# Splitting every fourth V load by partitions, 112 + 8 + 8, in a grouped-query attention block

## The chip, the core and the metric

One core of one Trainium2 chip runs the whole program in one launch. The metric is the device time of that launch in microseconds (us). A run that is over 1.5% above the fastest of its kernel counts as slow. A profiled execution is a little shorter than its timed run, because its span runs from the first to the last instruction (385.4 us where the time was 387.23).

In a profile, PE is the matmul engine, PEld its weight load, DVE and ACT the two elementwise engines, SP the engine that issues nearly all the loads here. Sixteen DMA engines move the data.

## The reference

```python
# B=32, Sq=4, D=1024, Hq=32, Hkv=4, Sk=2048, Dh=128, all bf16
q = (x @ wq).reshape(B, Sq, Hq, Dh).transpose(0, 2, 1, 3)
k = repeat(k_cache, 8, axis=1); v = repeat(v_cache, 8, axis=1)
p = softmax(einsum("bhqd,bhkd->bhqk", q, k) * Dh ** -0.5)
o = einsum("bhqk,bhkd->bhqd", p, v)
return o.transpose(0, 2, 1, 3).reshape(B, Sq, Hq * Dh) @ wo
```

For each of the 32 batches 2 MB of K and 2 MB of V must come in from HBM, and 16 MB of weights besides: 151 MB in all, each byte used once.

## The kernel before

Each batch's K and V go into one of three buffers. A load is issued on SP as soon as the batch three earlier has let its buffer go, so several loads are queued at any time. In a V load partition p takes 16 consecutive keys of each of the four kv heads: four pieces of 4 KB. In a K load it takes one piece of 16 KB.

```python
def load_k(b):
    p.dma("sp", lambda e: e.dma_start(
        K_sb[:, b % NKB, :, :], k_cache[b].rearrange("g (r t) d -> (g r) t d", r=R)),
        [("fill", b - NKB, NFILL - 1)] if b >= NKB else [], ("k", b), f"s_k{b % NKB}")

def load_v(b):
    src = v_cache[b].rearrange("g (p t) d -> p g (t d)", p=128)
    dst = V_sb[:, b % NVB, :, :, :].rearrange("p g t d -> p g (t d)")
    waits = [("pv", b - NVB)] if b >= NVB else []
    if b < B - 1:
        p.dma("sp", lambda e: e.dma_start(dst, src), waits, ("v", b), f"s_v{b % NVB}")
    else:
        for g in range(G):   # the last one in four pieces, by head
            p.dma("sp", ..., waits, ("v", b, g), f"s_vl{g}")
# ... cut ...
load_k(0)
load_k(1)
for b in range(B):
    if b + 2 < B:
        load_k(b + 2)
    load_v(b)
    if b in (2, 3, 4, 5):
        load_wo(b - 2)
# ... cut: Q projection; per batch K transposes, QK, softmax, PV, output projection ...
```

A load's semaphore gets one increment from each DMA engine that worked on it, when that engine's share has landed. The consumer waits for the full count, so it waits for the slowest engine.

## Time and profile before

| | before |
|---|---|
| time | 387.33 us (387.23 to 387.41, 3 runs) |
| bytes moved | 152.32 MB, mean 395 GB/s |
| loads' share of the 16 DMA engines | 96.1% of the span |
| PE / DVE / ACT busy | 73% / 71% / 54% |
| DMA in the chain of waits | 59% |

The lines are from the page of the kernel before: the span; two rows of the 40 slices (9.6 us each; a digit is a busy share in tenths, the second row is what the DMA engines moved); the SP queue's packets, MB and share of 16 engines; the head of the chain of waits; and the DMA issues with KB of one load and median us from issue to landing.

```profile
span 385.4 us, 12595 instructions
DMA  7999999999999999999999999999999999999930
GB/s 328 432 432 416 418 417 398 413 410 395 413 409 409 419 416 414 419 413 418 417 419 417 417 414 417 416 416 411 417 417 417 418 420 415 417 418 410 375 143 9
...
q1 hardware_dynamic: 27104, 151.49, 96.1%
q8 instruction: 46, 0.75, 0.8%
...
DMA 59%; PE 17%; ACT 13%; DVE 7%; issue 2%; SPq 1%
...
K_sb<-in_k_cache_dram SPq DMA_DIRECT2D x32, 2048.0 KB, 25.4
V_sb<-in_v_cache_dram SPq DMA_DIRECT2D x31, 2048.0 KB, 27.3
```

The DMA row is full from the second slice to the 38th, at 375 to 432 GB/s. No compute engine is near full. The kernel is bound by its loads, and a load is on the way for 25 us, five loads' time: the queue is deep.

Behind these lines lie the single records. A V load costs an engine 32 packets of 4 KB at 161 ns, a K load 8 packets of 16 KB at 615 ns (26.6 GB/s for one engine). The times of the 16 increments of each semaphore show that the engines drift apart: the first and the last are 1.8 us apart in the first K load and 9.7 us in the last one. Eight engines fall behind, one at a time, in steps of about 1.5 us. The q8 line has 46 instruction packets of 16 KB, about six for each of the eight, and I read those as the steps' cause. The times bear this out: the lags of the engines behind the first one, added up, grow from 11.1 us when 5 instruction packets had started to 72.7 us when 42 had, about 1.7 us for each. The increments do not name their engine.

### The profile page before, as it was taken

Reading aid. Unit: us, or ns where it says so; the run is one execution under the profiler, and the core shown is the slowest. Engines: PE = TensorE matmul, PEld = TensorE weight load, DVE = VectorE, ACT = ScalarE, POOL = GpSimd, SP = SyncE. Lnnn points to the kernel's source line nnn. Section 1 sums busy time; section 2 is a strip of 40 time slices with the busy share of each in tenths; the row PEclk is TensorE's granted clock in tenths of the full one; section 3 lists DMA queues with packets and bytes.
Section 4 is the critical chain, followed back from the end, with each engine's and each line's share of the span. In section 5 each row is a group of like instructions: output and inputs, shape, how many; then the busy total and the mean of one; then the engine's idle time right before and its main releaser. Section 6 shows DMA issues by size and latency. Waiting matters only on the chain.

```text
span 385.4 us, 12595 instructions
## 1 busy us (share of the span) xinstructions
PE 280.9 (73%) x5929; PEld 229.5 (60%) x5929; DVE 274.1 (71%) x299; ACT 208.5 (54%) x261; POOL 0.7 (0%) x6
## 2 busy tenths in 40 slices
PE   1876888676383967888767778877767888776756
PEld 1875766465282856666655566665645676565545
DVE  0017999683552984899888859998868859987850
ACT  1005777355161646676666627766646566666620
POOL 0000000000000000000000000000000000000000
PEclk9998999886976899999999999999999999999978
DMA  7999999999999999999999999999999999999930
GB/s 328 432 432 416 418 417 398 413 410 395 413 409 409 419 416 414 419 413 418 417 419 417 417 414 417 416 416 411 417 417 417 418 420 415 417 418 410 375 143 9
DMA packets 27251, 152.32 MB, mean 395 GB/s; under 512 B 1472, under 2 KB 1984, under 8 KB 22592
## 3 DMA queue, kind: packets, MB, share of 16 engines
q1 hardware_dynamic: 27104, 151.49, 96.1%
q8 instruction: 46, 0.75, 0.8%
q10 hardware_dynamic: 96, 0.03, 0.0%
q14 instruction: 5, 0.04, 0.0%
HBM read 151.26 MB, written 0.26 MB: 393 GB/s over the span
## 4 chain that ended last, share of the span: by engine, by line
DMA 59%; PE 17%; ACT 13%; DVE 7%; issue 2%; SPq 1%
DMA K_sb<-in_k_cache_dram 59%; ACT KT_sb L219 7%; ACT P_sb L285 6%; DVE KT_sb L217 4%; PE ps_r L207 4%; PE ps_r L248 3%; PE ps_r L296 3%; PE ps_r L225 3%; PE ps_s L240 3%; DVE mx L280 2%; PE ps_s L296 1%; DVE PT_sb L231 0%; SPq L129 0%; PE ps_r L271 0%; ACT oT_sb L275 0%
## 5 line engine op out<-in xcount | busy, mean ns | idle before, releaser
L207 PE MATMUL ps_r<-ident,K_sb 128*128 128x128 bf16 x2048 | 142.6, 229 | 66.0 <-DMA K_sb<-in_k_cache_dram 40.8
L217 DVE COPY KT_sb<-ps_r 128x1024 bf16<-128x1024 bf16 x128 | 148.0, 1216 | 40.0 <-PE ps_r L207 39.8
L207 PEld LDWEIGHTS ps_r<-ident,K_sb 128*128 128x128 bf16 x2048 | 125.7, 103 | 82.2 <-DMA K_sb<-in_k_cache_dram 41.9
L219 ACT ACTIVATE KT_sb<-ps_r 128x1024 bf16<-128x1024 bf16 x128 | 124.5, 1025 | 72.1 <-PE ps_r L207 72.0
L280 DVE TENSOR_REDUCE mx<-ps_s 128x1 f32<-128x2048 f32 x32 | 73.3, 2292 | 7.1 <-PE ps_s L240 4.6
L285 ACT ACTIVATE P_sb<-ps_s,negmx 128x2048 bf16<-128x2048 f32 x32 | 63.0, 1969 | 2.2 <-DVE negmx L281 2.1
L231 DVE COPY PT_sb<-ps_r 128x1024 bf16<-128x1024 bf16 x64 | 41.4, 686 | 16.7 <-PE ps_r L225 15.2
L248 PE MATMUL ps_r<-V_sb,PT_sb 128*32 128x128 bf16 x2048 | 36.7, 223 | 17.2 <-ACT KT_sb L219 12.8
L248 PEld LDWEIGHTS ps_r<-V_sb,PT_sb 128*32 128x32 bf16 x2048 | 31.0, 98 | 22.7 <-ACT KT_sb L219 19.4
L275 ACT ACTIVATE oT_sb<-ps_r 128x128 bf16<-128x128 bf16 x31 | 8.6, 277 | 55.6 <-PE ps_r L271 55.6
L225 PE MATMUL ps_r<-ident,P_sb 128*128 128x128 bf16 x512 | 35.1, 223 | 1.8 <-ACT P_sb L285 1.4
L240 PE MATMUL ps_s<-KT_sb,QT_sb 128*32 128x512 bf16 x512 | 34.3, 386 | 2.5 <-DVE KT_sb L217 1.7
L225 PEld LDWEIGHTS ps_r<-ident,P_sb 128*128 128x128 bf16 x512 | 29.4, 99 | 5.4 <-ACT P_sb L285 1.6
L240 PEld LDWEIGHTS ps_s<-KT_sb,QT_sb 128*32 128x32 bf16 x512 | 10.8, 96 | 13.3 <-issue 2.8
L187 DVE CAST QT_sb<-ps_r 128x512 bf16<-128x512 f32 x2 | 1.3, 686 | 22.4 <-PE ps_r L176 22.4
L265 ACT ACTIVATE o_sb<-ps_r,rinv 128x128 bf16<-128x128 f32 x31 | 11.4, 367 | 9.8 <-PE ps_r L248 9.8
L189 ACT ACTIVATE QT_sb<-ps_r 128x512 bf16<-128x512 f32 x2 | 1.1, 594 | 26.0 <-PE ps_r L176 26.0
L176 PE MATMUL ps_s<-P_sb,w_sb 128*128 128x128 bf16 x128 | 9.4, 232 | 7.2 <-DMA w_sb<-in_wq_dram 7.2
L296 PE MATMUL ps_r<-w_sb,oT_sb 128*32 128x256 bf16 x384 | 11.5, 273 | 2.6 <-issue 1.4
L176 PEld LDWEIGHTS ps_s<-P_sb,w_sb 128*128 128x128 bf16 x128 | 8.3, 105 | 7.8 <-issue 4.4
L296 PEld LDWEIGHTS ps_r<-w_sb,oT_sb 128*32 128x32 bf16 x384 | 10.0, 97 | 3.7 <-issue 2.5
L271 PEld LDWEIGHTS ps_r<-ident,o_sb 128*128 128x128 bf16 x31 | 3.0, 98 | 12.7 <-issue 12.7
(30 smaller groups left out, 58.9 us busy)
## 6 DMA issues: line engine op xcount, KB each, us to landing
K_sb<-in_k_cache_dram SPq DMA_DIRECT2D x32, 2048.0 KB, 25.4
V_sb<-in_v_cache_dram SPq DMA_DIRECT2D x31, 2048.0 KB, 27.3
w_sb<-in_wq_dram SPq DMA_DIRECT2D x4, 2048.0 KB, 14.8
w_sb<-in_wo_dram SPq DMA_DIRECT2D x4, 2048.0 KB, 24.7
V_sb<-in_v_cache_dram SPq DMA_DIRECT2D x4, 512.0 KB, 15.8
P_sb<-in_x_dram SPq DMA_DIRECT2D x1, 256.0 KB, 2.8
out_dram<-y_sb SPq DMA_DIRECT2D x14, 16.0 KB, 12.1
out_dram<-y_sb ACTq DMA_DIRECT2D x2, 16.0 KB, 1.6
```

The source lines that it names most:

```text
L176: p.op("pe", lambda e, kt=kt, h=h: e.matmul(ps_q(h), lhsT=w_sb[:, kt, h * Dh:(h + 1) * Dh], rhs=xT_sb[:, kt, :], start=(kt == 0 and h % 4 ...
L207: p.op("pe", lambda e, q=q, t=t: e.transpose(buf[:, q * 128:(q + 1) * 128], K_sb[:, b % NKB, t, :], ident[:, :]), waits + [("k", b), "iden ...
L217: p.op("dve", lambda e: e.tensor_copy(dst, src), waits, ("kt", b, f))
L219: p.op("act", lambda e: e.activation(dst, src, ACT.Copy), waits, ("kt", b, f))
L225: p.op("pe", lambda e, q=q: e.transpose(buf[:, q * 128:(q + 1) * 128], P_sb[:, (8 * f + q) * 128:(8 * f + q + 1) * 128], ident[:, :]), wai ...
L231: p.op("dve", lambda e: e.tensor_copy(PT_sb[:, 8 * f:8 * f + 8, :].rearrange("p t q -> p (t q)"), buf), [("ptf", i, f)] + ([("pv", i - 1)] ...
L240: p.op("pe", lambda e, c=c, g=g: e.matmul(ps_s[32 * g:32 * (g + 1), c * 512:(c + 1) * 512], lhsT=QT_sb[:, i, REP * g:REP * (g + 1), :], rh ...
L248: p.op("pe", lambda e: e.matmul(buf[32 * g:32 * (g + 1), 0:Dh], lhsT=PT_sb[:, t, 32 * g:32 * (g + 1)], rhs=V_sb[:, i % NVB, g, t, :], star ...
L265: p.op("act", lambda e: e.activation(o_sb[:, :], buf[:, 0:Dh], ACT.Copy, scale=rinv[:, i:i + 1]), [("pv", i), ("rinv", i)] + ([("oT", i - ...
L280: p.op("dve", lambda e: e.tensor_reduce(mx[:, i:i + 1], ps_s[:, :], AX.X, ALU.max), [("qk", i)], ("mx", i))
L285: p.op("act", lambda e: e.activation(P_sb[:, :], ps_s[:, :], ACT.Exp, bias=negmx[:, i:i + 1], scale=scale, accum_out=ssum[:, i:i + 1]), [( ...
L296: p.op("pe", lambda e, h=h, j=j: e.matmul(buf[32 * j:32 * (j + 1), 0:NC], lhsT=oT_sb[:, h, 32 * n:32 * (n + 1)], rhs=wo_sb[:, h, NC * j:NC ...
```

## The change

Its evident intent is to level that drift. The split pieces of 8 rows run on 8 DMA engines instead of 16, so in each split load these 8 engines get 9 partitions each and the other 8 get 7, in place of 8 and 8.

```diff
+        v_parts = {}
+
         def load_v(b):
 ...
             if b < B - 1:
-                p.dma("sp", lambda e: e.dma_start(dst, src), waits, ("v", b), f"s_v{b % NVB}")
+                parts = ((0, 112), (112, 120), (120, 128)) if b % 4 == 2 else ((0, 128),)
+                for n, (p0, p1) in enumerate(parts):
+                    p.dma("sp", lambda e, p0=p0, p1=p1: e.dma_start(dst[p0:p1, :, :], src[p0:p1, :, :]),
+                          waits, ("v", b, n), f"s_v{b % NVB}_{n}")
+                v_parts[b] = [("v", b, n) for n in range(len(parts))]
 ...
         def pe_pv(i):
-            waits = waits + [("pt", i, 0), ("pt", i, 1), ("v", i)]
+            waits = waits + [("pt", i, 0), ("pt", i, 1)] + v_parts[i]
```

## The prediction

> **What bounds the kernel now.** The loads. The page's DMA row is at 9 tenths from the second slice to the 38th, the SP queue fills 96.1% of the 16 engines' span, and 59% of the chain of waits is DMA (K loads). PE (73%), DVE (71%) and ACT (54%) have slack. Per engine, a V load is 32 packets of 4 KB at 161 ns (5.15 us) and a K load 8 packets of 16 KB at 615 ns.
>
> The 16 engines do not stay together. The trace holds the 16 increments of each load's semaphore. For the first K load they lie within 1.8 us; for the last V loads the last engine is 9.8 us behind the first: six engines within 0.3 us of the first, two about 2 us behind, eight 7.8 to 9.8 us behind. The eight fall back one at a time in steps of about 1.5 us, and the page lists 46 instruction packets (queue 8, 1.08 us each): about six for each of eight engines. A load has landed only when its slowest engine is done, so those eight set the pace. The end follows from them: the last K load lands at 358.6 us, the last V quarter at 373.9, the span ends at 385.4.
>
> **What the change does.** b = 2, 6, ..., 30: eight V loads. 112 partitions are 7 per engine instead of 8; each load of 8 partitions is one per engine on eight engines. The Trainium skill ("DMA: Bandwidth & Descriptors", on why a DMA increments its semaphore by 16) says HWDGE takes the lowest-numbered eight. So engines 0-7 get 9 partitions, 8-15 get 7. A partition is 4 x 161 ns = 0.64 us: eight times, 5.2 us more on 0-7 and 5.2 less on 8-15. Evidently the aim is to level the 9.8 us. The 16 more issues cost SP about 0.45 us each, off the path.
>
> *If the eight late engines are 8-15 and nothing else changes:* the mean lag is 4.7 us, so at best about 5 us comes off: 382-383 us, within 2%. If the late ones were 0-7, about 5 us are added.
>
> *What I expect to be larger:* the destination. The skill's "SBUF — State Buffer" (section on the DMA port swizzle) puts partitions 112-115, 116-119, 120-123, 124-127 on one write port each, of about 27 GB/s. This trace has 26.6 GB/s for one engine's 16 KB packet, so one engine fills such a port, but no run yet shows several engines on one. In the 128-partition load each engine has its own port. In a load of 8 partitions four engines write through one port: estimate 4 x 0.64 = 2.5 us, 3 us with the port's own engine, in place of 0.64. Two such loads, less one partition saved: 4.4 to 5.5 us per split load on engines 0-7, 35 to 44 us over eight, less the 8-10 us that they lead: +25 to +34 us, all on the path. The 112-partition load may also no longer match ports to engines. I hold this about 60% likely, with partial versions between.
>
> **Predicted:** 405 us, 80% range 382 to 420; faster over 2%: 0.03, within 2%: 0.43, slower: 0.54. The outcome has two modes (about 383, about 414).
>
> **What would show it.** Port sharing: 4 KB packets of several hundred ns in the eight stretches, DMA GB/s dipping there, eight engines landing some 5 us later after each split load, more PE wait on K and V. Pure levelling: packets stay at 161 ns, the spread of the last V loads falls from 9.8 to some 4 us, the last K lands near 354 us.
>
> **What would make it wrong.** Ports that take several engines at full rate; engines not in step, so that they pass a port one after another; the late eight not being 8-15.

## The result, and the profile after

| | before | after |
|---|---|---|
| time | 387.33 us | 485.97 us (485.21 to 486.05, 3 runs) |
| ratio | | 1.254 (95%: 1.251 to 1.257) |
| bytes moved, mean rate | 152.32 MB, 395 GB/s | 152.32 MB, 315 GB/s |
| PE's wait on K loads, on V loads | 40.8 us, 2.0 us | 57.8 us, 53.3 us |

A ratio here is the mean time of one kernel's fast runs over that of the other's in the same rounds, so it is not quite the ratio of the medians (e1 is an exception, see there). The change costs 98.6 us, far above the range that was predicted.

The same lines of the page after the change (a slice is now 12.1 us), then the issues of the split loads:

```profile
span 483.3 us, 12619 instructions
DMA  8999999999999999999999999999999999999540
GB/s 351 427 430 410 375 206 410 406 406 400 297 212 420 409 317 201 364 417 349 203 299 418 411 211 218 353 415 282 215 245 393 415 218 221 309 382 293 134 152 14
...
q1 hardware_dynamic: 27232, 151.49, 95.7%
q8 instruction: 46, 0.75, 0.7%
...
DMA 69%; PE 13%; ACT 7%; SPq 5%; DVE 4%; issue 1%
...
K_sb<-in_k_cache_dram SPq DMA_DIRECT2D x32, 2048.0 KB, 33.8
V_sb<-in_v_cache_dram SPq DMA_DIRECT2D x23, 2048.0 KB, 35.7
V_sb<-in_v_cache_dram SPq DMA_DIRECT2D x8, 1792.0 KB, 37.9
V_sb<-in_v_cache_dram SPq DMA_DIRECT2D x16, 128.0 KB
```

The bytes and the instruction packets are the same, and the loads' share of the engines is 95.7%, as before: the engines are not idle, they are slow. Every few slices the rate falls to about half, 201 to 221 GB/s, and between the early dips it is 400 to 430. Towards the end the dips run into one another.

PE's waits on loads, from the waits view (who waited for whom; us in total, times, longest us). Before:

```profile
PE ps_r L207 <- DMA K_sb<-in_k_cache_dram: 40.8, 18, 7.1
PE ps_r L248 <- DMA V_sb<-in_v_cache_dram: 2.0, 2, 1.4
```

After, with the same two lines of code now at 213 and 254:

```profile
PE ps_r L213 <- DMA K_sb<-in_k_cache_dram: 57.8, 16, 9.2
PE ps_r L254 <- DMA V_sb<-in_v_cache_dram: 53.3, 12, 6.8
```

PV now waits for V, which it hardly did. PE was granted a lower clock in this run (0.851 in the mean, 0.946 before), but it is busy for 65% of the span only and waits for data, so its clock is not what lengthens the run. The 5% of the chain at SPq are above all two issues of V loads that took SP 9.2 and 10.0 us; e3 below has as many issues, single ones of up to 9.4 us too, and loses nothing.

Two stretches in numbers, as the windows view gives them (us; then busy time of each engine with its count; the clock granted to PE; the DMA engines' share, which can pass 1 because records overlap; GB/s). The first stretch holds the split load b = 2, the second holds no split load. Before:

```profile
57.00:69.50 12.50, 9.91 (x237) 7.86 (x241) 12.18 (x14) 10.30 (x13) 0.00 (x0) 1.00 1.04 403
80.00:110.00 30.00, 16.55 (x306) 14.15 (x304) 14.88 (x18) 10.73 (x14) 0.00 (x0) 0.78 1.03 407
```

After:

```profile
57.00:76.00 19.00, 13.45 (x276) 10.49 (x277) 13.96 (x16) 10.38 (x13) 0.00 (x0) 0.83 1.05 256
80.00:110.00 30.00, 18.71 (x322) 16.41 (x322) 17.03 (x18) 12.82 (x16) 0.00 (x0) 0.72 1.03 406
```

The stretch without a split load is untouched (407 and 406 GB/s). The stretch with one goes from 403 to 256 GB/s at a full DMA share. From the packet records between about 56 and 72 us: the mean 4 KB packet took 328 ns in place of 164, and 82 of the load's 512 packets took over 400 ns, where before it was 1.

The K loads' semaphores give the loss split by split. The delay is that of the mean of a K load's 16 increments against the same load before; the spread is its last increment minus its first.

| after the split at b = | 2 | 6 | 10 | 14 | 18 | 22 |
|---|---|---|---|---|---|---|
| read at K load | 7 | 11 | 15 | 19 | 23 | 27 |
| delay of the mean, us | 7.1 | 16.6 | 27.4 | 38.7 | 52.8 | 68.2 |
| added by this split, us | 7.1 | 9.5 | 10.8 | 11.3 | 14.1 | 15.4 |
| spread, us (before) | 3.6 (3.5) | 4.7 (3.8) | 8.0 (5.4) | 11.2 (6.6) | 16.7 (6.9) | 18.7 (8.4) |

After the first split nothing more is lost until the next: K loads 5, 6 and 7 all have a delay of 7.1 us. Each of these six splits is dearer than the one before it, and the spread grows with it. (The splits at 26 and 30 have too few K loads after them to be read in this way.)

One more sum over all packet records closes the account. Take the time by which packets exceed their usual 88 ns (2 KB), 161 ns (4 KB) and 615 ns (16 KB), and divide by 16 engines:

| us per engine | 2 KB | 4 KB (V loads) | 16 KB (K and wq loads) | all |
|---|---|---|---|---|
| before | 0.5 | 3.5 | 1.2 | 5.2 |
| after | 2.3 | 56.5 | 37.7 | 96.5 |

Longer packets are 91.3 of the 97.9 us between the spans. Some 36.5 us of it sit in 16 KB packets, loads that the change does not touch.

### The profile page after: what moved, and what is told of

It reads as the page before. It is cut to its first block, busy times and chain, and to the rows that moved or that the text cites. A ratio compares the mean times of both kernels' runs of the same rounds, so it can differ in the third digit from the quotient of the medians.

```text
span 483.3 us, 12619 instructions
## 1 busy us (share of the span) xinstructions
PE 312.7 (65%) x5929; PEld 258.3 (53%) x5929; DVE 275.1 (57%) x299; ACT 208.4 (43%) x261; POOL 0.7 (0%) x6
## 2 busy tenths in 40 slices
DMA packets 27379, 152.32 MB, mean 315 GB/s; under 512 B 1600, under 2 KB 2112, under 8 KB 22720
## 3 DMA queue, kind: packets, MB, share of 16 engines
q1 hardware_dynamic: 27232, 151.49, 95.7%
## 4 chain that ended last, share of the span: by engine, by line
DMA 69%; PE 13%; ACT 7%; SPq 5%; DVE 4%; issue 1%
DMA K_sb<-in_k_cache_dram 39%; DMA V_sb<-in_v_cache_dram 25%; DMA w_sb<-in_wq_dram 5%; SPq L146 4%; ACT KT_sb L225 4%; ACT P_sb L291 3%; PE ps_r L213 3%; PE ps_r L254 3%; PE ps_r L231 3%; DVE KT_sb L223 2%; PE ps_s L246 2%; DVE mx L286 1%; PE ps_r L302 1%; PE ps_s L302 1%; PE ps_s L182 0%
## 5 line engine op out<-in xcount | busy, mean ns | idle before, releaser
L213 PE MATMUL ps_r<-ident,K_sb 128*128 128x128 bf16 x2048 | 152.8, 239 | 83.0 <-DMA K_sb<-in_k_cache_dram 57.8
L213 PEld LDWEIGHTS ps_r<-ident,K_sb 128*128 128x128 bf16 x2048 | 137.1, 109 | 97.6 <-DMA K_sb<-in_k_cache_dram 60.2
L237 DVE COPY PT_sb<-ps_r 128x1024 bf16<-128x1024 bf16 x64 | 42.4, 688 | 82.1 <-PE ps_r L231 80.8
L254 PE MATMUL ps_r<-V_sb,PT_sb 128*32 128x128 bf16 x2048 | 46.6, 257 | 65.3 <-DMA V_sb<-in_v_cache_dram 53.3
L286 DVE TENSOR_REDUCE mx<-ps_s 128x1 f32<-128x2048 f32 x32 | 73.3, 2292 | 11.7 <-PE ps_s L246 10.3
L254 PEld LDWEIGHTS ps_r<-V_sb,PT_sb 128*32 128x32 bf16 x2048 | 39.6, 116 | 70.7 <-issue 55.0
L231 PE MATMUL ps_r<-ident,P_sb 128*128 128x128 bf16 x512 | 44.2, 255 | 1.1 <-issue 0.6
L231 PEld LDWEIGHTS ps_r<-ident,P_sb 128*128 128x128 bf16 x512 | 38.0, 117 | 6.0 <-issue 3.3
L246 PE MATMUL ps_s<-KT_sb,QT_sb 128*32 128x512 bf16 x512 | 37.3, 409 | 2.4 <-DVE KT_sb L223 1.7
```

Source lines behind the costliest of these rows:

```text
L213: p.op("pe", lambda e, q=q, t=t: e.transpose(buf[:, q * 128:(q + 1) * 128], K_sb[:, b % NKB, t, :], ident[:, :]), waits + [("k", b), "iden ...
L231: p.op("pe", lambda e, q=q: e.transpose(buf[:, q * 128:(q + 1) * 128], P_sb[:, (8 * f + q) * 128:(8 * f + q + 1) * 128], ident[:, :]), wai ...
L237: p.op("dve", lambda e: e.tensor_copy(PT_sb[:, 8 * f:8 * f + 8, :].rearrange("p t q -> p (t q)"), buf), [("ptf", i, f)] + ([("pv", i - 1)] ...
L246: p.op("pe", lambda e, c=c, g=g: e.matmul(ps_s[32 * g:32 * (g + 1), c * 512:(c + 1) * 512], lhsT=QT_sb[:, i, REP * g:REP * (g + 1), :], rh ...
L254: p.op("pe", lambda e: e.matmul(buf[32 * g:32 * (g + 1), 0:Dh], lhsT=PT_sb[:, t, 32 * g:32 * (g + 1)], rhs=V_sb[:, i % NVB, g, t, :], star ...
L286: p.op("dve", lambda e: e.tensor_reduce(mx[:, i:i + 1], ps_s[:, :], AX.X, ALU.max), [("qk", i)], ("mx", i))
```

## The experiments

Theory P: the destination rows set which SBUF port an engine writes through (the Trainium skill's page "SBUF — State Buffer", the DMA port swizzle), and engines that share a port share its rate. A load of 128 partitions gives each engine a port of its own ("DMA: Bandwidth & Descriptors", "The descriptor swizzle"); the split pieces do not. The words "own port" and "two to a port" below are P's, from that page's table; no trace here names a port. Rivals: C, that more loads, semaphores and waits cost; N, that the load on 8 engines and the 9-to-7 imbalance cost; R, that reading these source rows, or a narrow load as such, costs whatever the destination.

| run | time, us | before in the same rounds, us | ratio (95%) |
|---|---|---|---|
| e3, three loads of 128 partitions | 387.18 | 386.94 | 1.001 (0.998 to 1.003) |
| e1, 112 + 16 | 465.64 (mean of its 2 fast runs) | 386.72 (mean) | 1.204 |
| e2, 64 + 64 | 465.78 (mean of its 3 fast runs) | 386.72 (mean) | 1.204 (1.200 to 1.209) |
| e4, extra 8-row loads, adjacent rows | 412.78 | 387.13 | 1.068 (1.063 to 1.074) |
| e5, the same, rows on the engines' own ports | 396.28 | 387.13 | 1.023 (1.018 to 1.027) |
| e6, the same, rows on other engines' ports | 408.73 | 387.13 | 1.056 (1.053 to 1.059) |
| e7, extra loads of 112 partitions | 421.25 | 387.18 | 1.088 (1.086 to 1.091) |
| e8, the same bytes in 128 partitions | 396.65 | 387.18 | 1.025 (1.022 to 1.028) |
| e9, the split at b = 2 alone | 393.74 | 387.18 | 1.019 (1.016 to 1.021) |
| e10, the split at b = 26 alone | 401.29 | 387.18 | 1.037 (1.035 to 1.039) |
| e11, extra 16-row loads, adjacent rows | 406.06 | 387.35 | 1.048 (1.045 to 1.051) |
| e12, the same, every eighth row | 402.37 | 387.35 | 1.040 (1.038 to 1.042) |

All twelve gave the right result. The other times are medians of four fast runs. In e1 two of the four runs were slow (475.04 and 471.83 us), in e2 one (471.82). The ratio for e1 is what the two fast runs, 463.53 and 467.74, give: 1.204, and two runs are too few for an interval.

### e3: three loads, but each of 128 partitions

```diff
-parts = ((0, 112), (112, 120), (120, 128)) if b % 4 == 2 else ((0, 128),)
+parts = ((0, 2), (2, 3), (3, 4)) if b % 4 == 2 else ((0, 4),)   # kv heads
-e.dma_start(dst[p0:p1, :, :], src[p0:p1, :, :])
+e.dma_start(dst[:, g0:g1, :], src[:, g0:g1, :])
```

> The same eight V loads are cut into three as in the change, but along the kv heads (2, 1, 1), so that every load keeps 128 partitions. Theory P (destination: several DMA engines write through one SBUF port and share its rate): 386 to 389 us, nothing is lost, since engines and partitions match as before. Theory C (three loads, three semaphores and three waits in place of one are what costs): about 486 us, as the change. Theory N (loads narrower than 128 partitions, on 8 engines, and the 9-to-7 imbalance): 386 to 389.

Measured 387.18 us against 386.94: nothing lost. The GB/s row of its page has no dip:

```profile
GB/s 331 427 430 417 417 419 398 411 412 394 410 412 406 420 416 419 414 415 416 417 419 418 419 411 418 413 424 408 416 417 418 416 419 417 418 415 412 375 140 9
```

The number of loads, semaphores and waits is not the cause; theory C falls.

### e1: 112 and 16 partitions, every engine still with 8

```diff
-parts = ((0, 112), (112, 120), (120, 128)) if b % 4 == 2 else ((0, 128),)
+parts = ((0, 112), (112, 128)) if b % 4 == 2 else ((0, 128),)
```

> The same eight V loads are cut into 112 and 16 partitions, both on 16 engines, so every engine carries 8 partitions as before and no load runs on 8 engines. Theory P: most of the loss stays, 425 to 490 us, since neither piece keeps one engine to one port (estimate: a 16-partition load puts four engines on each of four ports, 4 x 0.64 = 2.6 us in place of 0.64, and the 112-partition load adds 2 us or more). Theory N (imbalance, and the loads on 8 engines alone): 386 to 392. Theory C: two loads in place of three, about 435.

Measured 465.64 us in the fast runs, 78.9 us over before. Without any load on 8 engines and without any imbalance, 80% of the loss (78.9 of 98.6) is still there. Theory N falls as the main cause. The dips are those of the change:

```profile
GB/s 336 430 429 423 409 203 355 402 402 411 401 215 356 420 415 229 315 418 419 261 262 413 418 302 203 347 413 392 210 242 419 415 267 220 326 415 295 210 168 9
```

### e2: two halves of 64

```diff
-parts = ((0, 112), (112, 120), (120, 128)) if b % 4 == 2 else ((0, 128),)
+parts = ((0, 64), (64, 128)) if b % 4 == 2 else ((0, 128),)
```

> The same eight V loads are cut into two halves of 64 partitions, both on 16 engines, 4 partitions each. Theory P: each half reaches only 8 ports, so two engines share each port: a half takes 64 x 0.64 / 8 = 5.1 us in place of 2.6, 5 us more for each split load, 40 us over eight if the engines stay in step: 415 to 450. Theory N: 386 to 390. Theory C: two loads in place of three, about 435, told from P by the run cut along the heads.

Measured 465.78 us in the fast runs, 79.1 us over before, and above the 415 to 450 that I gave P. The first split behaves as P says: it delays the mean by 5.8 us (5 expected), and in its stretch 401 of 512 packets of 4 KB took between 280 and 400 ns; the median of the 512 is 314, about twice the usual 161. Since 256 of them belong to each half, both halves were slowed, the one in the lower 64 rows too. Two engines to a port fits that. Later splits cost up to 10 us and more, which P with engines in step does not give; e9 and e10 take that up.

### e4, e5, e6: the same small loads, three sets of destination rows

Here every V load stays whole. After each of the first 31 come two extra loads of 8 rows of 4 KB, into a scratch tile that nothing reads; together they are the bytes of the change's 8-row loads. The three kernels differ in the destination rows alone.

```diff
+X_sb = sbuf("X_sb", [128, TV * Dh], BF16)
+def load_extra(b):                      # called after load_v(b), b < 31
+    s = b % 4
+    for n in range(2):
+        p.dma("sp", ... e.dma_start(X_sb[ROWS, :], src[112 + 8 * n:120 + 8 * n, 0, :]),
+              [("x", b - 4, n)] if b >= 4 else [], ("x", b, n), f"s_e{s}{n}")
+# e4: ROWS = 64 + 16*s + 8*n : 72 + 16*s + 8*n     (adjacent)
+# e5: ROWS = 32*n + s : 32*n + s + 29 : 4          (every fourth, lower 64)
+# e6: ROWS = 64 + 32*n + s : 64 + 32*n + s + 29 : 4  (every fourth, upper 64)
```

> The kernel before, every V load whole, plus after each of the first 31 V loads two extra loads of 8 partitions x 4 KB (engines 0 to 7) into a scratch tile that nothing reads: together the bytes of the change's small loads. The 8 destination rows are adjacent, in the upper 64 partitions, so four engines share a port, which is another engine's own. Theory P: 62 loads, each 4 to 5 x 0.16 = 0.64 to 0.8 us on engines 0 to 7, 40 to 50 us in all less the 8 to 10 us that these engines lead: 415 to 430 us. Rival R (the cost is in a load on 8 engines itself, or in reading these HBM rows, whatever the destination): this and the two spread ones are equally slow. Rival Z (small loads are harmless, the loss sits in the 112-partition load): 387 to 390.

> As the packed one, the same source rows, sizes, engines and waits; only the destination rows are every fourth of 32 in the lower 64 partitions, so that each of the engines 0 to 7 should write its own port. Theory P: 62 x 0.16 = 10 us more on engines that lead by 8 to 10 us: 387 to 390 us. Rival R: as slow as the packed one.

> As the last, but every fourth of 32 rows in the upper 64 partitions: eight engines on eight ports, each of which is also another engine's own. Theory P: a pair shares a port for 0.32 us in place of 0.16: up to 62 x 0.16 = 10 us more on the engines that are last already, and none if they happen to stall then: 390 to 400 us, between the two others. Rival R: as slow as the packed one.

Measured: 412.78, 396.28 and 408.73 us. The packets beyond their usual time, summed as above:

| us per engine | 2 KB | 4 KB | 16 KB |
|---|---|---|---|
| e4, adjacent | 2.0 | 10.4 | 11.0 |
| e5, own ports | 0.6 | 3.5 | 1.9 |
| e6, other engines' ports | 1.9 | 10.1 | 8.8 |
| before | 0.5 | 3.5 | 1.2 |

The GB/s row of e4, from its page:

```profile
GB/s 334 431 432 410 394 391 381 388 402 381 415 389 392 394 392 392 398 394 394 390 389 396 385 394 391 395 397 394 391 396 391 394 391 395 397 392 389 364 136 8
```

And of e5:

```profile
GB/s 332 435 423 415 418 416 403 409 409 397 412 410 421 414 414 415 420 414 410 418 420 417 412 419 411 418 420 415 414 415 420 410 413 414 414 421 388 336 50 8
```

Same source rows, same sizes, same number of loads and waits: with rows spread over the lower 64, packets are as short as before and the rate is mostly 410 to 420 GB/s; with adjacent rows it is mostly 380 to 400. The difference of 16.5 us is the destination's. Rival R falls for these loads. The sizes are not as P had them: e4 lies just under its 415 to 430 us, and e6, with two engines to a port, was to lie at 390 to 400 us and came out close to e4.

Two limits of this comparison. First, e5 differs from the two others also in the half: its rows are in the lower 64, theirs in the upper 64. That writing to the other half is what costs was not tested by itself; e2, whose lower half was slowed too, and e12 below, whose rows lie in both halves (7.6 and 6.2 us of excess in 4 KB and 16 KB packets), speak against it as the whole cause. Second, the packets of e4 do not look as P in step would have them, 640 ns each. Over 400 ns were 31 of its 4 KB packets, where before it was 40 and in e5 41. Instead 2,225 took 175 to 225 ns (3 in e5, none before): the loss is a mild stretch spread over many packets, those of whole loads included. That the rows decide is shown; that a port's rate is divided is not.

And e5 itself missed: 387 to 390 was expected, because the eight engines were taken to lead by 8 to 10 us. They do not all lead. The increments show it. These are the 16 landings of V load 29 in e5 and the 8 of the extra load queued right behind it, in us, each extra load's landing 0.18 to 0.21 after that of its engine's V share:

```
V 29   357.44 357.67 361.84 361.87 361.88 361.90 363.26 363.30
       363.42 363.51 363.74 364.42 364.86 365.37 370.90 372.52
extra  363.44 363.48 363.95 364.61 365.04 365.55 371.10 372.72
```

The two engines that are last of all sixteen belong to the eight of the extra load. Matched by these times, of the other eight engines six land between 361.84 and 363.51, where six of the late ones land in the kernel before (its late eight: 361.85 to 363.67). So of the eight late engines six are outside the set that an 8-row load runs on, and two are inside it. Already at V load 2 two of the five late engines are inside (their extra landings, 65.04 and 65.24, follow V landings at 64.83 and 65.01). Some 10 us of work (62 x 161 ns) on that set moved the last landing of the last K load by 9.1 us and the time by 9.2 us: there was no lead to use up.

### e7 and e8: the 112-partition load by itself

Again every V load is whole. After every second one comes an extra load of 258 KB into scratch.

```diff
+X_sb = sbuf("X_sb", [128, 2, N], BF16)
+def load_extra(b):                      # called after load_v(b), b even
+    s = (b // 2) % 2
+    p.dma("sp", ... e.dma_start(X_sb[0:ROWS, s, :], src[0:ROWS, 0, 0:N]),
+          [("x", b - 4)] if b >= 4 else [], ("x", b), f"s_e{s}")
+# e7: ROWS = 112, N = 1152        e8: ROWS = 128, N = 1008
```

> The kernel before, every V load whole, plus after every second V load one extra load of 112 partitions x 2304 B into a scratch tile (16 of them, 4.1 MB). To be read against the run with 128 partitions x 2016 B, the same bytes. Theory P (a 112-partition load no longer gives each engine its own port): its packets take 1.5 to 2 times as long and other engines' packets in the same stretch too; 5 to 20 us slower than its control, so 402 to 417 us. Rival S (only the loads of 8 or 16 adjacent rows cost): as its control, 396 to 398.

> Control of the last: 16 extra loads of 128 partitions x 2016 B, the same 4.1 MB, at 415 GB/s about 10 us: 396 to 398 us under both theories, no packet slower than before.

Measured: 421.25 against 396.65 us. The same 4.1 MB cost 24.6 us more in 112 partitions than in 128, over the top of my range; the control is within its own. The GB/s row of e7, from its page:

```profile
GB/s 337 434 426 410 385 417 369 396 411 362 406 409 360 421 359 414 377 401 380 383 391 377 412 359 415 354 416 358 405 378 390 376 382 380 385 391 366 370 201 9
```

And of its control e8:

```profile
GB/s 331 434 424 417 417 418 399 409 408 395 412 409 410 416 415 415 411 418 415 418 420 412 418 414 414 414 417 412 416 417 419 413 415 414 422 410 413 403 207 9
```

The change moves 14.7 MB in loads of 112 partitions (8 x 1.835 MB). If the loss goes with the bytes, that is an estimate of 24.6 x 14.7 / 4.1 = 88 us, near e1's 78.9. The agreement may be chance: the cost of a byte is not constant (e9, e10), and e1 holds 2.1 MB in pieces of 16 rows besides. The extra load's own packets of 2304 B are only a part of the loss: they took 120 ns in the mean, with the fastest twentieth at 93 or less, which is 1.3 times and not the 1.5 to 2 times that I expected. The 4 KB packets of the whole V loads beside them lost 12.5 us per engine and the 16 KB packets 11.7, where before lost 3.5 and 1.2. Both are the loss of loads that share the stretch.

### e9 and e10: one split, early or late

```diff
-parts = ((0, 112), (112, 120), (120, 128)) if b % 4 == 2 else ((0, 128),)
+parts = ((0, 112), (112, 120), (120, 128)) if b == 2 else ((0, 128),)    # e9
+parts = ((0, 112), (112, 120), (120, 128)) if b == 26 else ((0, 128),)   # e10
```

> The change's split at b = 2 alone. In the changed kernel the first split moved the mean landing of the next K load by 7.1 us, the later ones by 10 to 15. Theory G (the cost of a split grows with how far the engines have been spread, above all by earlier splits): 394 to 395 us here. Rival (each split costs the same 12 us on average): 399.

> The change's split at b = 26 alone, where the engines of the kernel before are 8 us apart from the instruction fetches but no earlier split has spread them. If earlier splits made the late ones dear: 394 to 396 us, as at b = 2. If any spread does, that of the fetches too: 398 to 402 us.

Measured: 393.74 and 401.29 us, 6.6 and 14.1 us over before; the first is just under the 394 to 395 of theory G, the second within its range. In e10 nothing had been split earlier; the engines were 8 us apart from their own drift alone. So the growth of the cost does not need earlier splits. The GB/s row of e10 has one dip, three slices wide:

```profile
GB/s 341 419 438 410 418 416 410 399 406 405 408 412 415 417 417 418 415 415 417 417 417 417 415 417 412 417 414 418 416 417 416 409 202 212 300 416 413 382 132 8
```

The packet account says where the extra comes from. In e9 the 16 KB packets lose 1.8 us per engine (before: 1.2), in e10 7.2; the 4 KB packets 8.1 and 10.9 (before: 3.5). My reading: when the engines are together, nearly all of them are in the split load at once; when they are 8 us apart, some are still in the K load before it or already in the one after it, and those are slowed too. One difference besides the spread was not separated: at b = 2 the load right behind the split one is a wo load of 2 KB packets (they lose 1.9 us per engine in e9, 0.5 before), at b = 26 it is a K load.

### e11 and e12: sixteen rows, four or two to a port

As e4, with one extra load of 16 rows on all 16 engines after each of the first 31 V loads.

```diff
+        p.dma("sp", ... e.dma_start(X_sb[ROWS, :], src[112:128, 0, :]), ...)
+# e11: ROWS = 64 + 16*s : 80 + 16*s  (adjacent)     e12: ROWS = s : s + 121 : 8
```

> The kernel before, plus after each of the first 31 V loads one extra load of 16 partitions x 4 KB on all 16 engines, one partition each, into 16 adjacent scratch rows of the upper 64 (2.0 MB in all, 5 us at 415 GB/s). Theory P: four engines on each of four ports, 0.64 us in place of 0.16 on every engine, 15 us over 31 loads, and something more on the ports' owners: 405 to 420 us. Rival R (source rows or narrow loads cost, not the destination): as the strided one.

> As the last, same source rows and engines, but the destination is every eighth row of 128, so 16 rows lie on eight ports, two on each. Theory P: 0.32 us in place of 0.16, 5 us over 31 loads besides the 5 us for the bytes: 394 to 404 us, clearly below the adjacent one. Rival R: equal to the adjacent one.

Measured: 406.06 and 402.37 us, both in the ranges given, and the intervals of the ratios do not overlap. The order is P's. The distance is not: 3.7 us where "15 in place of 5" would give 10. So this pair supports that destination rows matter on 16 engines too, and shows that my arithmetic of engines in step is only good for the order. It alone would not have decided against R; e4 against e5 does.

## Why the prediction was wrong

It said 405 us with a range of 382 to 420; it was 485.97. "Slower" had 0.54.

*What bounds the kernel: right.* The loads do, before and after, and the added time is nearly all on the path: 91.3 of 97.9 us are longer packets.

*The mechanism: right in kind.* The signs that it named came: 4 KB packets of several hundred ns, GB/s dips in the stretches of split loads, more PE wait on K and V. e4 against e5 shows that the destination rows of an 8-row load decide. But packets of several hundred ns hardly occur where 8-row loads run alone (e4); e1 and e2, without any, have them by the hundred (224 and 401 of 512 between 280 and 400 ns at the first split).

*The step that failed: the paragraph on the destination, which put the cost in "a load of 8 partitions", "4.4 to 5.5 us per split load on engines 0-7", and left the 112-partition load to one sentence without a number ("may also no longer match ports to engines").* That sentence held the large term. e1 has no 8-row loads and keeps 78.9 of 98.6 us; its 16-row pieces explain only a part, since as many bytes in extra loads of 16 adjacent rows cost 18.7 us (e11), some 5 of them for the bytes. e7 against e8 puts 24.6 us on 4.1 MB of 112-partition loads. The 8-row loads' own share is smaller than the 35 to 44 us estimated: packed small loads of about the same bytes cost 25.6 us (e4), of which 9.2 are there with rows on the engines' own ports (e5).

*A second term was taken as constant.* The first split cost 7.1 us where the estimate had 4.4 to 5.5, but the sixth cost 15.4. A single split costs 6.6 us early and 14.1 us late (e9, e10). The prediction multiplied a cost for engines in step by eight, and did not count what a slowed stretch does to the K loads around it, which took 36.5 us of the loss.

*A third step was a credit that did not exist: "less the 8-10 us that they lead".* I also gave "at best about 5 us" for the pure levelling if the late eight are engines 8-15. Two of the late eight are inside the set that an 8-row load runs on (e5), so more work on that set moves the last landing out at once. From this I infer that levelling by 8-row loads would not have reached 382 us in this kernel. It was not run as a levelling without shared ports; e5 shows the part of it that adds work.

*What stays open.* That the wide pieces (112, 64) lose time at the SBUF ports is inferred: their packets stretch (a median of 314 ns in e2), and e3 and e8 exclude the number of loads and the bytes. No run kept their source rows and changed only their destination, and the trace does not say which engine writes which row of a 112-partition load. No version that beats both kernels came out of this: every split into fewer than 128 partitions, and every extra load, moved the end out.

## What to carry to other kernels

In a kernel bound by its loads, keep every large load at 128 partitions and cut it along the free dimension if it must be cut: three loads of 128 partitions cost nothing here (e3), while 112 + 16 or 64 + 64 in an eighth of the loads cost 20%. Before shifting work between DMA engines, find out which engines are late and which engines a narrow load uses, for instance by a small extra load queued right behind a whole one and the landing times of both. And when a resource is shared for a moment, ask who else is in it: the loads before and after paid over a third of this bill.

## What the Trainium skill lacked or had wrong

- "DMA: Bandwidth & Descriptors", "Rules for kernel authors", advises for using all 16 engines a dimension that is a multiple of 16, ideally the 128 partitions, and says of two transfers to disjoint partition halves that they serialize, so don't bother. It does not say there that a load of fewer than 128 partitions on 16 engines can be far slower; lower rates of single transfers to 64 and 16 partitions stand on the page "SBUF — State Buffer". What neither page has is 112 partitions, also a multiple of 16, and what such loads do to the loads queued around them: 24.6 us more for 4.1 MB (e7, e8), 79.1 us for eight loads cut in halves (e2).
- The same page, "The descriptor swizzle", gives the engine of each partition for 128 partitions and refers other shapes to how the engine count is chosen. Which rows each engine gets of 112 partitions, and so which ports meet, is not stated there; e1, with 112 + 16 rows, lost 78.9 us.
- "SBUF — State Buffer", the DMA port swizzle: the order of e4, e5 and e6 fits its table of ports (usual packets with own ports, 10.4 and 10.1 us of excess in 4 KB packets with shared ones), though four and two to a port hardly differ. The page (section "SBUF: two separate sides") names these ports as a place of contention when several DMA engines write to them, but gives no size for it; here loads that were not part of the small ones lost 8.8 to 11.0 us in 16 KB packets.
- "Runtime: NRT & Kernel Launch", "Instruction fetch mechanics", calls the cost of a fetch mostly hidden. Here 46 packets of 16 KB run on the DMA engines of the loads, and from their times I take the steps of about 1.5 us by which eight engines fall up to 9.8 us behind, in a kernel whose loads are its limit. The page does not say which engines carry the fetches; e5 finds six of the late ones outside the set of an 8-row load and two inside it.
